# Value products of the last block in two 64-row halves, with a second PSUM bank of sums

## The chip, the cores and the metric

The kernel runs on one core of a Trainium2 chip. The metric is the device time of one execution in microseconds. The engines are named as in the profile: PE (TensorE, matrix products; PEld are its weight loads), DVE (VectorE), ACT (ScalarE), POOL (GpSimd) and SP (which issues DMAs). PSUM, into which PE writes, has eight banks; one bank holds 128 partitions of 512 float32 values, one tile of this kernel.

## The reference

Two attentions over 2048 positions with 32 heads of 18 columns, each with its own input and weights; their outputs stand side by side. A looks at eight positions, two apart, behind each position; B looks at all positions. The change touches B:

```python
qkv = (x @ wqkv).reshape(B, S, 3, H, Dh).transpose(2, 0, 3, 1, 4)
q, k, v = qkv[0], qkv[1], qkv[2]
scores = jnp.einsum("bhqd,bhkd->bhqk", q, k) * scale
p = _softmax(scores, axis=-1)
o = jnp.einsum("bhqk,bhkd->bhqd", p, v)
return o.transpose(0, 2, 1, 3).reshape(B, S, D) @ wo
```

All in float32. Many products of the kernel split their operands into a high and a low part of the faster type float32r and add three products; the value products (p times v) are plain float32, which makes two weight loads and two matmuls of one product.

## The kernel before

**Blocks and steps.** B's attention goes by groups of four heads (`g`, eight of them), blocks of 512 queries (`b`, four) and tiles of 128 keys (`kt`, 16). A step is one (g, b, kt): for each of the four heads, `score` (L219) makes a 128x512 tile of scores, keys on partitions (L226), and ACT makes its exponentials `e` (L232). While they last, maxima of later blocks are taken beside the scores (L156 on PE, L163 on DVE); for the last block there are none left to take.

**Value products.** `weigh` (L694) multiplies the exponentials with the values: for each head `i`, a product (L697) of the 128 keys' 19 columns (18 of the value and a column of ones, which sums the weights) with `e`, into partitions 32i to 32i+18 of the tile `po`. So four products stand in four column tiles of the array, and po collects 16 steps (`start` at kt 0, `stop` at kt 15). Partitions 32i+19 to 32i+31 are never written by PE; po is cleared once, far ahead (L658). In the last group and its last blocks, `weigh` is called for two steps at a time, at odd kt. At kt 15 it calls `finish`.

**What follows a block.** `finish` (L702) copies po to `o` on ACT (L706); for the last block it calls `closing` (L770) in place of that. In the last group the division by the sums is made on DVE: transpose in squares of 32, reciprocal, multiply, transpose back (`shortly` L739 for blocks 1 and 2, `inverse` L756 in `closing`). `closing` first makes the product that still lacks (`first(3, b, 1)`, L976), then two times `inverse` from po into o over 256 columns, and for each 128 columns a high part (ACT L779) and a low part (POOL L780); `end` multiplies with wo (L976), adds what had been summed before (L1036) and stores.

**Output products.** In the last block, PE also makes outputs of earlier blocks and parts of this block's. They are *quarters*: `sum_of` (L1009) lets `beside` (L987) make 288 columns for 128 positions in two halves of 64 rows, taken in turns and each with a PSUM bank of its own, 15 products a half (12 where the newest heads still lack), all at L1001. DVE then copies the first half's bank (L1020) and adds the second's (L1021). The list `waiting` holds them: one is made before `weigh` is called in a step, and another in even steps after the scores.

**Banks.** `bank()` gives the next bank of a ring: banks 0 to 3 for scores, 4, 5 and 6 for everything else, po is the eighth. A bank that is given again waits for the last reader of its tile. A quarter takes two banks of "else"; `first` takes one and keeps it until `end`.

**Order.** From L270 on the order of each engine's instructions is the order in which the program writes them. Nothing is moved; only waits on tiles hold an instruction back, and then everything behind it on its engine.

Of the kernel before, what the change touches and what calls it, by code (L numbers as in the profile page):

```python
# [7 lines left out]
F32 = mybir.dt.float32  # L8
F32R = mybir.dt.float32r
BF16 = mybir.dt.bfloat16  # L10
AF = mybir.ActivationFunctionType
# [11 lines left out]
NG = H // 4  # L23
NT = S // 128
NB = S // 512
# [34 lines left out]
def two_attentions(ctx: ExitStack, tc, xa, wa, woa, xb, wb, wob, out):  # L60
# [5 lines left out]
    nc = tc.nc  # L66
# [6 lines left out]
    p_bank = ctx.enter_context(tc.tile_pool(name="p_bank", bufs=1, space=PSUM))  # L73
# [3 lines left out]
    rings = {"all": list(range(7)), "scores": [0, 1, 2, 3], "else": [4, 5, 6]}  # L77
    ring = "all"

    def bank(kind=None):  # L80
        r = rings[kind or ring]
        r.append(r.pop(0))
        return p_bank.tile([128, 512], F32, name=f"bank{r[-1]}")
# [11 lines left out]
    po = p_po.tile([128, 512], F32, name="po")  # L95
# [141 lines left out]
    vs = {}  # L237
# [98 lines left out]
    with (tc.tile_pool(name="x", bufs=1, side="right") as xp,  # L336
# [103 lines left out]
        if True:  # L440
# [236 lines left out]
            es = []  # L677
# [13 lines left out]

    work = ctx.enter_context(tc.tile_pool(name="work", bufs=1, reuse_waits="tile"))
    ring = "else"
    def weigh(*steps):  # L694
        for g, b, kt, es in steps:
            for i in range(4):
                nc.tensor.matmul(po[32 * i : 32 * i + 19], vs[g][:, kt, 19 * i : 19 * i + 19], es[i],  # L697
                                 start=kt == 0, stop=kt == NT - 1)
        if kt == NT - 1:
            finish(g, b)  # L700

    def finish(g, b):  # L702
        o = work.tile([128, 512], F32, name="o", bufs=2)
        if g == NG - 1 and b == NB - 1:
            return closing(b, o, work.tile([128, 512], F32, name="rec", bufs=1))
        nc.scalar.activation(o, po, AF.Copy)  # L706
        den = work.tile([128, 16], F32, name="den", bufs=2)
        rec = work.tile([128, 512], F32, name="rec", bufs=1)
        parts = []

        def room():
            if g == NG - 1 and b == 0:

                parts[:] = [ap(work.tile([128, 4, 128], F32R, name=f"at{i}", bufs=1), (1, 512)) for i in range(2)]
            else:
                n = work.tile([128, 2, 512], F32R, name="n", bufs=1)
                parts[:] = n[:, 0], n[:, 1], n
            return parts

        if g == NG - 1 and b > 0:  # L720
            return shortly(b, o, rec, *room()[:2])

        def store():
            if g < NG - 1:
                load(do[:, g, :, 512 * b : 512 * b + 512].rearrange("i p n -> p i n"), parts[2].bitcast(F32))
            else:
                plan(step, full(b, parts))

        for at, f in ((1, lambda: load(den, o[DH:128:32])),
                      (8, lambda: nc.vector.reciprocal(den, den)),  # L730
                      (9, lambda: load(drec[g, b].rearrange("i (p n) -> (i p) n", n=16), den)),
                      (13, lambda: load(rec, rows(drec[g, b], (512, 4), (0, 32), (1, 512)))),
                      (18, lambda: nc.gpsimd.tensor_mul(o, o, rec)),  # L733
                      (19, lambda: nc.gpsimd.tensor_copy(room()[0], o)),
                      (20, lambda: nc.gpsimd.tensor_sub(parts[1], o, parts[0])),
                      (26, store)):
            later(at, f)
# [18 lines left out]
    def inverse(src, turned, cols, o):  # L756

        nc.vector.transpose(turned[:, cols], src[:, cols])
        divided(turned[:, cols])
        nc.vector.transpose(o[:, cols], turned[:, cols])  # L760

    def divided(square):

        n = square.shape[1] // 32
        inv = work.tile([128, 16], F32, name="den", bufs=2)[:, :n]
        each = ap(square, (32, n), (1, DH + 1))
        nc.vector.reciprocal(inv, ap(square[:, DH:], (32, n)))
        nc.vector.tensor_mul(each, each, ap(inv, (1, n), (0, DH + 1)))

    def closing(b, o, rec):  # L770

        n = work.tile([128, 2, 512], F32R, name="n", bufs=1)
        first(3, b, 1)
        for t in range(4):
            if t % 2 == 0:
                inverse(po, rec, slice(128 * t, 128 * t + 256), o)
            cols = slice(128 * t, 128 * t + 128)
            hi, lo = n[:, 0, cols], n[:, 1, cols]
            nc.scalar.activation(hi, o[:, cols], AF.Copy)  # L779
            nc.gpsimd.tensor_sub(lo, o[:, cols], hi)  # L780
        for t in range(4):
            end(t, b, (n[:, 0], n[:, 1]))
# [188 lines left out]
    def some(ps, t, h, c, hi, lo, start, stop):  # L971
        pos, cols = slice(128 * t, 128 * t + 128), slice(288 * h, 288 * h + 288)
        n = hi.shape[0]
        whi, wlo = wo["b"][c]
        for k, (a, w) in enumerate(((hi, whi), (hi, wlo), (lo, whi))):
            nc.tensor.matmul(ps, a[:, pos], w[:n, cols], start=start and k == 0, stop=stop and k == 2)  # L976
# [46 lines left out]
    def first(t, b, h):  # L1023
        sums[t, b, h] = bank()[:, :288]
        for c in range(4):
            some(sums[t, b, h], t, h, c, *olds[b][c], c == 0, False)
# [17 lines left out]
    def end(t, b, new):  # L1044
        for h in range(2):
            half_end(t, b, h, new)
        load(out[512 * b + 128 * t : 512 * b + 128 * t + 128, D:], ys[t, b])
# [75 lines left out]
    while step < ALL:  # L1123
        n, kt = divmod(step, NT)
        g, b = divmod(n, NB)
        places = positions(min(4 if behind() > 0 else 3, total - sum(given)))
        es = []
        for h in range(4):

            if inside and h == (3 if 3 in places else 2):  # L1130
                inside.pop(0)()
            es.append(score(g, b, kt, h, h in places))
        for fs in (behind_scores, outside):
            while fs:
                fs.pop(0)()

        paired = paired or kt % 2 == 0 and sum(given) == total
        for _ in range(1 if paired and step < ALL - 2 else len(waiting)):
            if waiting:
                waiting.pop(0)()  # L1140
        if ready and (kt % 2 == 0 or not paired):
            weigh(ready.pop(0))
        ready.append((g, b, kt, es))
        if paired and kt % 2:
            weigh(*ready)
            ready.clear()
        due()

        if len(waiting) > (0 if not paired else 2 if kt % 2 else len(waiting)):
            waiting.pop(0)()  # L1150
        step += 1
# [24 lines left out]
```

## Time and profile before

| | us |
|---|---|
| median of 3 runs | 1642.11 |
| lowest and highest run | 1640.54, 1644.94 |
| span of the profiled execution, first to last instruction | 1639.3 |
| busy in that span: PE, DVE, ACT, POOL | 1629.1, 1395.2, 1221.8, 959.4 |

The page gives the profiled execution's span and no whole time for it. A row of a view names line, engine, operation and tiles (written <- read); then, in a timeline, start and duration, and in brackets how long the engine had been idle and what released it. An `x4` merges four neighbours of one kind, with the duration of their union. Groups give busy time, mean nanoseconds of one, and idle time before them. "issue" stands for a wait that no semaphore explains. A matmul of 512 columns is shown with its whole way through the array, so neighbours overlap, and the distance between starts is what one costs.

### The profile page before, as it was taken

The page shows a single profiled execution, that of the slowest core. Times are in us where ns is not written, and L with a number is a line of the kernel's source. Part 1 is how long each engine was busy: PE and PEld are TensorE (multiplying, and loading weights), DVE is VectorE, ACT ScalarE, POOL GpSimd, SP SyncE. Part 2 cuts the span into 40 slices and gives each one's busy share as a digit, 9 for nine tenths or more (in the row PEclk, how much of TensorE's full clock was granted, in tenths as well). Part 3 has the DMA queues.
Part 4 walks back from the last instruction along what each step waited for, and adds up shares of the span by engine and source line. Part 5 has one row for each costly group of instructions (what it writes and reads, how often), then busy time and mean ns, then how long its engine had stood idle before and what let it go on. Part 6 is the DMA issues. An engine that isn't in the chain of part 4 may idle for free.

```text
span 1639.3 us, 33789 instructions
## 1 busy us (share of the span) xinstructions
PE 1629.1 (99%) x12906; PEld 952.7 (58%) x12906; DVE 1395.2 (85%) x2366; ACT 1221.8 (75%) x2419; POOL 959.4 (59%) x792
## 2 busy tenths in 40 slices
PE   9999999999999999999999999999999999999998
PEld 7999889999433444344344444344344344344676
DVE  5199999999899989989889989889889989888533
ACT  6424432111899998998998998998998998998554
POOL 2306642210365995994994994994995996930000
PEclk9999999999999999999999999999999999999999
DMA  8937954522222352164146135332632242033201
GB/s 250 238 116 204 266 158 140 136 86 90 46 64 58 75 139 82 41 139 109 39 101 150 35 95 121 90 83 69 121 97 65 51 125 62 21 115 130 95 38 59
DMA packets 186050, 172.01 MB, mean 105 GB/s; under 512 B 119152, under 2 KB 132976, under 8 KB 184160
## 3 DMA queue, kind: packets, MB, share of 16 engines
q1 hardware_dynamic: 181024, 158.31, 35.4%
q0 software_dynamic: 4032, 10.63, 3.1%
q8 instruction: 101, 1.65, 0.5%
q10 hardware_dynamic: 832, 0.92, 0.2%
q14 instruction: 61, 0.50, 0.1%
HBM read 96.94 MB, written 71.90 MB: 103 GB/s over the span
## 4 chain that ended last, share of the span: by engine, by line
PE 95%; DMA 2%; DVE 1%; POOL 1%; issue 0%; ACT 0%; SPq 0%; POOLq 0%; ACTq 0%; DVEq 0%
PE po L697 30%; PE bank L226 25%; PE bank L319 14%; PE bank L156 13%; PE bank L1001 7%; PE bank L256 5%; DMA raw<-xa 1%; POOL xlo L367 1%; DVE mx L163 1%; DMA dqk<-olo 0%; DMA dqk<-ohi 0%; PE bank L471 0%; DMA more<-xa 0%; DVE am L852 0%; DMA out<-y 0%
## 5 line engine op out<-in xcount | busy, mean ns | idle before, releaser
L163 DVE TENSOR_REDUCE mx<-bank 128x1 f32<-128x512 f32 x2048 | 1287.7, 684 | 142.9 <-PE bank L156 114.9
L232 ACT ACTIVATE e<-bank 128x512 f32<-128x512 f32 x2048 | 1059.9, 613 | 90.0 <-PE bank L226 50.3
L156 PE MATMUL bank<-ks,qs 54*128 54x512 f32 x2048 | 750.0, 422 | 1.1 <-DVE mx L163 0.9
L226 PEld LDWEIGHTS bank<-qs,ks 56*128 56x128 f32 x2048 | 331.1, 185 | 453.2 <-ACT e L232 423.0
L226 PE MATMUL bank<-qs,ks 56*128 56x512 f32 x2048 | 580.2, 425 | 0.0
L697 PE MATMUL po<-e,v 128*19 128x512 f32 x4096 | 537.4, 599 | 0.0
L156 PEld LDWEIGHTS bank<-ks,qs 54*128 54x128 f32 x2048 | 340.2, 184 | 9.7 <-DVE mx L163 4.7
L697 PEld LDWEIGHTS po<-e,v 128*19 128x19 f32 x4096 | 70.6, 97 | 182.0 <-issue 171.2
L834 POOL TENSOR_TENSOR pr<-aq,akv 128x1024 f32<-128x1024 f32 x72 | 158.4, 2201 | 15.5 <-PE bank L226 13.0
L877 POOL TENSOR_TENSOR pr<-lg,akv 128x1024 f32<-128x1024 f32 x72 | 158.3, 2198 | 0.6
L838 POOL TENSOR_TENSOR pr<-pr 128x1024 f32<-128x1024 f32 x64 | 152.4, 2382 | 5.0
L647 ACT ACTIVATE ohi<-bank 128x512 f32<-128x512 f32 (+1 forms) x56 | 30.4, 596 | 150.1 <-issue 115.2
L319 PE MATMUL bank<-xhi,ahi 64*128 64x512 f32 (+1 forms) x448 | 114.5, 387 | 0.0
L319 PE MATMUL bank<-xhi,alo 64*128 64x512 f32 (+1 forms) x448 | 113.5, 387 | 0.0
L319 PE MATMUL bank<-xlo,ahi 64*128 64x512 f32 (+1 forms) x448 | 113.1, 388 | 0.1
L878 POOL TENSOR_TENSOR pr<-pr 128x512 f32<-128x512 f32 x72 | 92.3, 1282 | 5.6
L367 POOL TENSOR_TENSOR alo<-raw,ahi 128x512 fp32r<-128x512 f32 (+1 forms) x14 | 17.6, 1257 | 121.5 <-ACT ahi L366 87.8
L459 POOL TENSOR_TENSOR olo<-olo,ohi 128x512 fp32r<-128x512 f32 x36 | 46.1, 1293 | 67.3 <-ACT ohi L458 61.5
L733 POOL TENSOR_TENSOR o<-o,rec 128x512 f32<-128x512 f32 x29 | 37.3, 1286 | 53.9 <-DMA rec<-drec 47.5
L319 PEld LDWEIGHTS bank<-xhi,ahi 64*128 64x128 f32 (+1 forms) x448 | 65.8, 181 | 1.4
L319 PEld LDWEIGHTS bank<-xhi,alo 64*128 64x128 f32 (+1 forms) x448 | 64.9, 182 | 1.3
L319 PEld LDWEIGHTS bank<-xlo,ahi 64*128 64x128 f32 (+1 forms) x448 | 64.4, 182 | 1.9 <-POOL xlo L367 0.5
(197 smaller groups left out, 1795.5 us busy)
## 6 DMA issues: line engine op xcount, KB each, us to landing
do<-n SPq DMA_DIRECT2D x28, 512.0 KB
da<-ohi SPq DMA_DIRECT2D x52, 256.0 KB
akv<-da SPq DMA_DIRECT2D x64, 175.5 KB
out<-y SPq DMA_DIRECT2D x32, 288.0 KB
qs<-dqk SPq DMA_DIRECT2D x30, 288.0 KB
ks<-dqk SPq DMA_DIRECT2D x30, 288.0 KB
at<-dao SPq DMA_DIRECT2D x64, 128.0 KB
rec<-drec SPq DMA_DIRECT2D x29, 256.0 KB
```

Of the source, the lines that this page charges most:

```text
L156: nc.tensor.matmul(ps, qs[at, b, p, 128 * t : 128 * t + 128], ks[at, p, 512 * k : 512 * k + 512], start=True, stop=True)
L163: nc.vector.tensor_reduce(mx[:, r, p, t, k : k + 1], ps, axis=AX.X, op=ALU.max)
L226: nc.tensor.matmul(ps, ks[at, p, 128 * kt : 128 * kt + 128], qs[at, b, p], start=True, stop=True)
L232: nc.scalar.activation(e, ps, AF.Exp, scale=SCALE)
L256: nc.tensor.matmul(ps, a, b, start=c == i == 0, stop=c == 4 and i == 1)
L319: nc.tensor.matmul(ps, a, b, start=start, stop=stop)
L697: nc.tensor.matmul(po[32 * i : 32 * i + 19], vs[g][:, kt, 19 * i : 19 * i + 19], es[i], start=kt == 0, stop=kt == NT - 1)
L834: nc.gpsimd.tensor_mul(pr, ap(st["q"][:, 2 * c], (SUB, 2), (0, W), (1, SUB)), window(st["k"], c))
L838: nc.gpsimd.tensor_add(st["pr"], st["pr"], pr)
L877: nc.gpsimd.tensor_mul(at, ap(st["lg"], (0, 2), (SUB, W), (1, SUB)), window(st["v"], c))
L878: nc.gpsimd.tensor_add(at[:, :, :4], at[:, :, :4], at[:, :, 4:])
L1001: nc.tensor.matmul(ps, a, b, start=start, stop=stop)
```

## The change

In the last block of the last group (`last`), each value product is made as two, one of rows (keys) 0 to 63 and one of rows 64 to 127. The first goes to po, the second to a second tile of sums at the same partitions. That tile is bank 6: at the first call for this block it is taken out of the ring "else", which keeps two banks, and is cleared by DVE. In `closing`, ACT copies po to o, DVE adds the second tile to o, and `inverse` reads o where it read po. In all other blocks the loop over `(po, *other_po)` has one turn with all 128 rows, as before.

```diff
+    other_po = []
     def weigh(*steps):
         for g, b, kt, es in steps:
+            last = g == NG - 1 and b == NB - 1
+            if last and not other_po:
+                rings["else"].remove(6)
+                other_po.append(p_bank.tile([128, 512], F32, name="bank6"))
+                nc.vector.memset(other_po[0], 0.0)
             for i in range(4):
-                nc.tensor.matmul(po[32 * i : 32 * i + 19], vs[g][:, kt, 19 * i : 19 * i + 19], es[i],
-                                 start=kt == 0, stop=kt == NT - 1)
+                for r, to in enumerate((po, *other_po)):
+                    at = slice(64 * r, 64 * r + 64) if last else slice(0, 128)
+                    nc.tensor.matmul(to[32 * i : 32 * i + 19], vs[g][at, kt, 19 * i : 19 * i + 19], es[i][at],
+                                     start=kt == 0, stop=kt == NT - 1)
...
         first(3, b, 1)
+        nc.scalar.activation(o, po, AF.Copy)
+        nc.vector.tensor_add(o, other_po[0], o)
         for t in range(4):
             if t % 2 == 0:
-                inverse(po, rec, slice(128 * t, 128 * t + 256), o)
+                inverse(o, rec, slice(128 * t, 128 * t + 256), o)
```

## The prediction

> **What bounds the kernel now.** I read the page first: span, engines, share of the chain.
>
> ```profile
> span 1639.3 us, 33789 instructions
> PE 1629.1 (99%) x12906; PEld 952.7 (58%) x12906; DVE 1395.2 (85%) x2366; ACT 1221.8 (75%) x2419; POOL 959.4 (59%) x792
> PE 95%; DMA 2%; DVE 1%; POOL 1%; issue 0%; ACT 0%; SPq 0%; POOLq 0%; ACTq 0%; DVEq 0%
> ```
>
> PE is both the busiest engine and 95% of the chain, so a microsecond that PE waits or works more is a microsecond of time. The change touches the last block only, so next I asked for the value products (L697) from its first one on, and for the chain in one pair of its steps and at its end.
>
> ```profile
> L697 PE MATMUL po<-e,v x128: 592/592/607, 1571.8 to 1627.7; 128*19 128x512 f32 x128
> ```
>
> ```profile
> 1612.43 1.84 PE po L697 x16
> 1614.27 0.66 PE bank L226 x2
> 1614.93 1.99 PE bank L1001 x29
> 1616.92 0.49 PE bank L226 x4
> 1617.41 2.32 PE bank L1001 x29
> ...
> 1624.71 1.78 PE bank L976 x12
> 1626.49 1.96 PE po L697 x16
> ```
>
> The 64 products of the block are 128 PE instructions (two passes each), in 8 calls of `weigh` that take two steps each: 16 instructions, 1.84 us. A pair of steps is a chain of PE alone: `weigh`, four scores (L226), one output quarter (L1001), four scores, a second quarter. The second quarter takes 2.32 us where the first takes 1.99; the cause of that matters below.
>
> **The value products themselves.** PE's weight loads around two of the calls, behind the last product of the quarter before the first of them:
>
> ```profile
> 1619.44 0.29 PE L1001 MATMUL bank<-qs,n 64*128 64x288 f32 x1
> ...
> 1619.66 0.14 PEld L697 LDWEIGHTS po<-e,v 128*19 128x19 f32 x8 [0.16 <-issue]
> 1620.10 0.12 PEld L697 LDWEIGHTS po<-e,v 128*19 128x19 f32 x4 [0.31 <-issue]
> 1620.53 0.12 PEld L697 LDWEIGHTS po<-e,v 128*19 128x19 f32 x4 [0.31 <-issue]
> 1621.50 0.30 PEld L226 LDWEIGHTS bank<-qs,ks 56*128 56x128 f32 x4 [0.85 <-issue]
> ...
> 1626.42 0.13 PEld L697 LDWEIGHTS po<-e,v 128*19 128x19 f32 x8 [0.16 <-issue]
> ...
> 1628.26 0.19 PEld L976 LDWEIGHTS bank<-qs,pr 126*128 126x128 f32 x1 [0.85 <-issue]
> ```
>
> Four tiles of 32 columns run beside each other, one pass every 0.43 us (1620.10 to 1620.53), four passes a call. The change makes eight instructions per pass: four column tiles in two halves of 64 rows. Each half moves as many columns as the full depth did, so what counts is whether the halves run beside each other. No row shows that for these tiles. The nearest: L1001 is made of 64-row halves, 30 instructions of 288 columns in 1.99 us, 0.133 us a pair, while 12 full-depth ones of the same width (L976) take 1.78, 0.148 each. Two halves cost what one full product costs. So I take the passes as unchanged, plus the start of four more tiles: four loads of 0.10 us end within 0.12, so some 7 ns a tile, 0.03 us a call, **+0.2** for eight calls. Bounds: below, a half passes in half the time (rival 3, -6.9); above, the halves run one after the other, 16 steps x 2 passes x 0.43 = +13.8. Between them lies issue: L1001's 60 instructions in 1.99 us are 33 ns each, and a call will have 64, 2.12 us for 1.84 now, +2.3 in all.
>
> The Trainium skill ("TensorE: Matmul & The Clock Gate", measured speedup vs the span model) has a figure against the change: four row tiles of 512 columns gave 3.07 times one tile's rate, not 4. Worked out from it as an estimate, the 14.7 us of eight calls would take 4/3.07 of that, +4.5 us, and the sum would be +12.9; the L1001 and L976 rows show no such loss for two halves.
>
> **Drains.** Around a call PE's loads stop: 0.16 us before, 0.85 after. Scores after `weigh` take 0.66 us, after a quarter 0.49, so leaving costs about 0.17; entering costs 0.09 (1619.44 to 1619.66 is 0.22, against 0.133 between L1001's pairs). If halves of 64 rows beside halves of 64 rows needed no drain, 7 of 8 calls would save 0.26: -1.8. But at 1626.42 and 1628.26 `weigh` stands between L976 products, which use the array's depth as it does (126 rows) and differ from it in columns alone, and the idle times are the same 0.16 and 0.85. A change of columns alone drains too, and 64x128 to 64x32 is that. I take **0**, and keep -1.8 as the lower end.
>
> **The memset, once.** The new sums' bank 6 is cleared on DVE when the first call (1571.78) is written, and PE's second product needs it. What DVE has in its queue then:
>
> ```profile
> 1571.67 0.77 DVE L752 STREAM_TRANSPOSE o<-rec 128x256 f32<-128x256 f32 x2
> 1571.78 0.14 PEld L697 LDWEIGHTS po<-e,v 128*19 128x19 f32 x8 [0.16 <-issue]
> ...
> 1572.37 0.42 DVE L1020 COPY y<-bank 128x288 f32<-128x288 f32 x1
> ...
> 1572.89 0.46 DVE L1021 TENSOR_TENSOR y<-bank,y 128x288 f32<-128x288 f32 x1
> ```
>
> ```profile
> 1575.53 0.46 DVE L1020 COPY aohi<-bank 128x288 f32<-128x288 f32 x1 [2.18 <-PE bank L1001]
> ```
>
> ```profile
> L658 DVE MEMSET po<- x1: 485/485/485, 55.5 to 55.5; 128x512 f32 x1
> ```
>
> The order is written by hand: transposes of the block before, both evictions of the quarter just made, then the memset. L1021 ends at 1573.35; the memset of the same shape took 0.485, so bank 6 is clear at about 1573.87 and PE goes on at 1573.93 (a DVE end reaches PE after 0.05, next part). The call would have started at 1571.78: **+2.15**. The first half-product of po runs meanwhile, but the seven other tiles need their passes all the same. Behind the wait stand the rest of the call, a quarter and the scores, so ACT's exponentials come later too; DVE has 2.18 us of idle time behind it, so nothing is late on that side. Bounds: 1.6 if the memset gets ahead of L1021, 2.4 with slower hand-offs.
>
> **The ring of banks, eight times.** `rings["else"].remove(6)` leaves two banks for the quarters, and a quarter takes two. Between two quarters with only scores between them:
>
> ```profile
> 1609.65 0.46 DVE L1020 COPY y<-bank 128x288 f32<-128x288 f32 x1 [3.58 <-PE bank L1001]
> ...
> 1609.91 0.65 PE L1001 MATMUL bank<-qs,wohi 64*128 64x288 f32 x2
> 1610.16 0.18 PEld L1001 LDWEIGHTS bank<-qs,wohi 62*128 62x128 f32 x1 [0.29 <-DVE y L1020]
> ...
> 1610.21 0.46 DVE L1021 TENSOR_TENSOR y<-bank,y 128x288 f32<-128x288 f32 x1
> ```
>
> ```profile
>   PEld bank L1001: 2.3, 8
> ```
>
> With three banks the second quarter's first half has a free bank (start 1609.91); its second half needs the bank that L1020 empties: 1610.11, and PE goes on at 1610.16, 0.05 later. That is the missing third of a microsecond in the 2.32. The last row is the same wait summed, asked of L1020 from 1573.6 to 1624.9: 8 times, 0.29 each. With two banks the first half needs the bank of L1020 and the second half that of L1021, which ends at 1610.67 instead of 1610.11. Each of the eight waits grows by 0.56: **+4.5**. Where a `weigh` stands between quarters, its 1.84 us cover both evictions (1.0 us); without that cover those would wait as well. The `first` that follows a quarter directly takes one bank:
>
> ```profile
> 1624.25 0.46 DVE L1020 COPY y<-bank 128x288 f32<-128x288 f32 x1 [3.59 <-PE bank L1001]
> ...
> 1624.64 0.19 PEld L976 LDWEIGHTS bank<-qs,pr 126*128 126x128 f32 x1 [0.24 <-issue]
> ```
>
> Its bank comes free at 1624.71, PE at 1624.76 for 1624.64: **+0.1**. Bounds of the ring: 0 if the banks don't come round as I read it, 5.5 with a refill after each stall.
>
> **The end.** Now DVE transposes po itself. Afterwards ACT copies po to o, then DVE adds bank 6, and the transposes read o.
>
> ```profile
> 1564.77 0.60 ACT L706 ACTIVATE o<-po 128x512 f32<-128x512 f32 x1 [2.52 <-issue]
> ```
>
> ```profile
> 1628.48 0.45 DVE L758 STREAM_TRANSPOSE rec<-po 128x256 f32<-128x256 f32 x1 [3.21 <-PE po L697]
> ```
>
> ```profile
> L163 DVE TENSOR_REDUCE mx<-bank 128x1 f32<-128x512 f32 x2048 | 1287.7, 684 | 142.9 <-PE bank L156 114.9
> ```
>
> The copy starts about where the transpose does (1628.48) and takes 0.60. The add is 128x512 out of PSUM: 0.68 by L163, 0.81 by L1021's 0.46 for 288 columns scaled; I take 0.69, nearer the same shape. With two hand-offs of 0.05 the transposes start 1.4 us later. ACT has nothing queued ahead; behind the add stand the transposes, and everything that follows waits for them: **+1.4** (1.2 to 1.7).
>
> **The sum.** 0.2 + 0 + 2.15 + 4.5 + 0.1 + 1.4 = +8.35 us on a span of 1639.3. The median of the runs, 1642.11, lies 2.8 above that span (the page gives no whole time for the profiled execution); I let what lies around the span stand: 1642.1 + 8.4 = 1650.5.
>
> **Rivals.**
> 1. The halves do not fully run beside each other. For it: no row shows eight tiles of two halves in two-pass products. Against: the L1001 halves. It gives more than the issue bound, up to one half after the other: 1642.1 + 8.4 + 2.3 to 13.8, so 1653 to 1664. The chance is 0.12.
> 2. One of the two waits is not there (the memset is done in time, or the ring gives no wait more): +6.2 or +3.8, so 1648.3 or 1645.9. For it: the profile shows neither wait as it will be. Against: DVE works in order, and the eight waits are in the trace. Chances 0.04 and 0.06.
> 3. Not slower: a pass of a 64-row half takes 0.21 us in place of 0.43. For it: L226's 64-row pairs move 512 columns in 0.245 (four in 0.49). It would save 32 passes x 0.215 = 6.9 of the 8.4: 1643.6. It decides from 0.32 a pass (8.4 - 3.5 = 4.9). Against: L976 at full depth moves its columns as fast as half pairs do, so depth isn't what makes a value pass slow; the two passes per product are. Chance 0.05.
>
> **How the numbers follow.** My forecast holds 0.73: with its bounds (drains gone -1.8, issue +2.3) 1648.5 to 1653. Leaving out most of rival 1 (0.1) and rival 3 (0.05), the range for 8 in 10 is 1645.5 to 1656. What can be told from no change is 0.3%, 4.9 us, so slower begins at 1647.0. Slower: the forecast, rival 1 and the first case of rival 2, less 0.03 for the scatter of the medians, 0.86; the same: the second case of rival 2, most of rival 3 and that scatter, 0.11; faster: 0.03, for rival 3 with drains and a wait gone as well.
>
> **What would show it.** Right: 256 instructions of L697's line in the last block in two banks with eight starts within some 50 ns and passes still 0.43 apart; a wait of PE of about 2 us for a MEMSET at the block's first call; eight waits of L1001 of about 0.85 put down to L1021; the first transpose of the end 1.4 us further behind the last value product. Wrong: calls much over 1.9 us (rival 1) or under 1.5 (rival 3), scores after a call in 0.49 (no drain), waits that still name L1020.

## The result and the profile after

The changed kernel takes 1648.58 us (median of 5 runs, 1647.62 to 1649.96) against 1642.11 before (1639.87 to 1644.94): a ratio of 1.0044, 95% interval 1.0031 to 1.0058, so 5 to 9.5 us slower. The spans of the two profiled executions differ by 8.5 us. The page of the changed kernel, span and engines:

```profile
span 1647.8 us, 34049 instructions
PE 1633.5 (99%) x13034; PEld 949.7 (58%) x13034; DVE 1396.6 (85%) x2368; ACT 1222.3 (74%) x2420; POOL 959.1 (58%) x792
```

PE has 128 matmuls more, and its busy time grew by 4.4 us of the 8.5. That is no measure of the work added: the page of experiment 1, which adds no matmul, has 1632.6 us busy, 3.5 more than before, so a part of what PE waits is shown as busy. The value products of the last block (`weigh`'s matmul is L706 here), asked of their line over that stretch:

```profile
L706 PE MATMUL po<-e,v x128: 589/589/604, 1571.7 to 1635.0; 64*19 64x512 f32 x128
...
L706 PE MATMUL bank<-e,v x128: 589/589/603, 1573.9 to 1635.0; 64*19 64x512 f32 x128
```

The split is made: 256 instructions of 64 rows, half of them into the second bank. Two things can be read off the starts alone. The first and the last product of po start 63.3 us apart where it was 55.9, and the second bank's first product comes 2.2 us after po's.

**The first call.** The timeline of DVE and PE around it, in order of start:

```profile
1571.65 0.11 PEld L706 LDWEIGHTS po<-e,v 64*19 64x19 f32 x2 [0.16 <-issue]
1571.65 1.03 PE L706 MATMUL po<-e,v 64*19 64x512 f32 x2
...
1572.77 0.46 DVE L1032 TENSOR_TENSOR y<-bank,y 128x288 f32<-128x288 f32 x1
...
1573.33 0.48 DVE L702 MEMSET bank<- 128x512 f32 x1
...
1573.87 0.09 PEld L706 LDWEIGHTS bank<-e,v 64*19 64x19 f32 x1 [2.11 <-DVE bank L702]
```

PE makes one product of po (the x2 are its two passes), then stands until the memset is done, and the memset stands behind the add of the quarter before.

**Between quarters.** One place, the counterpart of the one shown before (the L1020 and L1021 of before are L1031 and L1032):

```profile
1607.69 0.46 DVE L1031 COPY y<-bank 128x288 f32<-128x288 f32 x1 [3.58 <-PE bank L1012]
...
1608.21 0.18 PEld L1012 LDWEIGHTS bank<-qs,wohi 64*128 64x128 f32 x1 [0.36 <-DVE y L1031]
...
1608.26 0.46 DVE L1032 TENSOR_TENSOR y<-bank,y 128x288 f32<-128x288 f32 x1
...
1608.77 0.18 PEld L1012 LDWEIGHTS bank<-qs,wohi 62*128 62x128 f32 x1 [0.38 <-DVE y L1032]
```

The second quarter's first half now waits for the copy, its second half for the add: PE goes on 0.05 us behind the end of L1032, not of L1031. The chain of waits of the changed kernel shows the same as steps of DVE in what was a chain of PE alone (start, duration, what):

```profile
1613.56 2.03 PE bank L1012 x30
1615.59 0.46 DVE y L1031
...
1616.14 0.47 DVE y L1032
...
1616.65 2.26 PE bank L1012 x27
```

**The calls themselves.** PE's weight loads around one call, and the starts of PE's matmuls in its first two passes:

```profile
1618.84 0.09 PEld L706 LDWEIGHTS po<-e,v 64*19 64x19 f32 x1 [0.16 <-issue]
...
1619.29 0.10 PEld L706 LDWEIGHTS po<-e,v 64*19 64x19 f32 x1 [0.29 <-issue]
...
1619.72 0.10 PEld L706 LDWEIGHTS po<-e,v 64*19 64x19 f32 x1 [0.29 <-issue]
...
1620.71 0.30 PEld L226 LDWEIGHTS bank<-qs,ks 56*128 56x128 f32 x4 [0.85 <-issue]
```

```profile
1618.85 0.60 PE L706 MATMUL po<-e,v 64*19 64x512 f32 x1
...
1618.89 0.60 PE L706 MATMUL bank<-e,v 64*19 64x512 f32 x1
1619.29 0.59 PE L706 MATMUL po<-e,v 64*19 64x512 f32 x1
...
1619.34 0.59 PE L706 MATMUL bank<-e,v 64*19 64x512 f32 x1
```

Passes are 0.43 us apart, as with full depth, with eight tiles in each that start within 50 ns. The idle times on both sides are 0.16 and 0.85, as before: 64-row halves beside 64-row halves did not save the drain.

**The end.** DVE's timeline behind the last call:

```profile
1636.37 0.69 DVE L784 TENSOR_TENSOR o<-bank,o 128x512 f32<-128x512 f32 x1 [4.00 <-ACT o L783]
1637.09 0.45 DVE L767 STREAM_TRANSPOSE rec<-o 128x256 f32<-128x256 f32 x1
```

The last call ends (next PE start) at 1635.50, so the transposes start 1.59 us behind it; before it was 1628.48 behind 1628.26, 0.22.

**An account of the last block.** The part of the kernel ahead of the block is the same code in all of them, save for the step or two in which experiments 2, 4, 5 and 6 begin, but it ends at different times in different executions: the first call starts anywhere from 1569.7 to 1574.9 us in the ten profiles of this study. So I read the experiments from that start to the end of the span, cut at the starts of the calls and of the instruction behind each (PE's timeline, us):

| kernel | first call | 7 other calls | between calls | behind the last | sum |
|---|---|---|---|---|---|
| before | 1.84 | 12.90 | 41.74 | 11.01 | 67.49 |
| changed | 4.08 | 13.07 | 46.70 | 12.31 | 76.16 |
| e1_ring_only | 1.84 | 12.90 | 46.35 | 11.00 | 72.09 |
| e2_clear_early | 1.87 | 13.06 | 46.97 | 12.30 | 74.21 |
| e3_no_add | 4.08 | 13.06 | 46.70 | 10.98 | 74.83 |
| e4_two_engines_evict | 3.03 | 13.07 | 42.41 | 12.23 | 70.73 |
| e5_costs_undone | 1.87 | 13.07 | 42.41 | 12.16 | 69.50 |
| e6_before_two_engines | 1.84 | 12.90 | 41.67 | 10.89 | 67.30 |
| e7_halves_in_turn | 4.05 | 13.06 | 46.71 | 12.30 | 76.13 |
| e8_one_more_on_dve | 4.21 | 13.06 | 46.38 | 12.30 | 75.95 |

Changed less before: 2.24 + 0.17 + 4.96 + 1.30 = 8.67 us. Each row is one execution, but stretches that a kernel leaves as they are repeat closely: 46.70, 46.70 and 46.71 between the calls of the changed kernel and of experiments 3 and 7.

### The profile page after: what moved, and what is told of

Read it like the earlier page. It is cut to its first block, busy times and chain, and to the rows that moved or that the text cites. A ratio compares the mean times of both kernels' runs of the same rounds, so it can differ in the third digit from the quotient of the medians.

```text
span 1647.8 us, 34049 instructions
## 1 busy us (share of the span) xinstructions
PE 1633.5 (99%) x13034; PEld 949.7 (58%) x13034; DVE 1396.6 (85%) x2368; ACT 1222.3 (74%) x2420; POOL 959.1 (58%) x792
## 4 chain that ended last, share of the span: by engine, by line
PE 92%; DMA 2%; DVE 2%; POOL 2%; issue 1%; ACT 0%; SPq 0%; POOLq 0%; DVEq 0%; ACTq 0%
PE po L706 30%; PE bank L226 25%; PE bank L156 13%; PE bank L319 12%; PE bank L1012 7%; PE bank L256 5%; DMA raw<-xa 2%; POOL xlo L367 1%; DMA dqk<-olo 1%; DVE mx L163 1%; POOL olo L459 0%; PE bank L471 0%; DVE y L1032 0%; DVE y L1031 0%; PE bank L706 0%
## 5 line engine op out<-in xcount | busy, mean ns | idle before, releaser
L226 PEld LDWEIGHTS bank<-qs,ks 56*128 56x128 f32 x2048 | 331.2, 185 | 453.3 <-ACT e L232 423.0
L226 PE MATMUL bank<-qs,ks 56*128 56x512 f32 x2048 | 580.1, 425 | 0.0
L706 PE MATMUL po<-e,v 128*19 128x512 f32 (+1 forms) x4096 | 538.6, 599 | 0.0
L706 PEld LDWEIGHTS po<-e,v 128*19 128x19 f32 (+1 forms) x4096 | 71.1, 96 | 180.9 <-issue 170.4
L319 PEld LDWEIGHTS bank<-xlo,ahi 64*128 64x128 f32 (+1 forms) x448 | 63.3, 182 | 2.4 <-POOL xlo L367 0.5
```

The source lines that it names most:

```text
L226: nc.tensor.matmul(ps, ks[at, p, 128 * kt : 128 * kt + 128], qs[at, b, p], start=True, stop=True)
L319: nc.tensor.matmul(ps, a, b, start=start, stop=stop)
L706: nc.tensor.matmul(to[32 * i : 32 * i + 19], vs[g][at, kt, 19 * i : 19 * i + 19], es[i][at], start=kt == 0, stop=kt == NT - 1)
```

## The experiments

The ratio of each experiment is to runs of the kernel before that were taken beside it, not to the 1642.11 of above: their medians are 1640.61 us (18 runs) for experiments 1 to 4 and 1640.67 us (21 runs) for 5 to 8.

**1. The ring alone.** The kernel before, which loses bank 6 and does nothing with it:

```diff
         for g, b, kt, es in steps:
+            if g == NG - 1 and b == NB - 1 and 6 in rings["else"]:
+                rings["else"].remove(6)
```

> The kernel before, with bank 6 taken out of the ring at the last block's first value products and nothing else. Theory (waits): each of the eight waits between neighbouring quarters grows from 0.29 to 0.85 us and names the add L1021 in place of the copy L1020, and the one ahead of the single product sums grows by 0.12, so the span is 4.6 us over the 1639.3 of before, about 1643.9. If the third of a microsecond by which one quarter of the changed kernel came later still is part of the ring, it shows here too (4.9). Rival (the halves are what costs): no change, within 0.5 us.

Measured: 1645.47 us, ratio 1.0029 (1.0017 to 1.0040); the last block 72.09, 4.60 more than before, all of it between the calls. One place between two quarters, from the timeline of DVE and PE, and then who waited for the add, asked of its line (L1023 in this kernel) and of L1021 in the kernel before:

```profile
1604.50 0.46 DVE L1022 COPY y<-bank 128x288 f32<-128x288 f32 x1 [3.56 <-PE bank L1003]
1605.02 0.18 PEld L1003 LDWEIGHTS bank<-qs,wohi 64*128 64x128 f32 x1 [0.37 <-DVE y L1022]
...
1605.07 0.46 DVE L1023 TENSOR_TENSOR y<-bank,y 128x288 f32<-128x288 f32 x1
...
1605.58 0.18 PEld L1003 LDWEIGHTS bank<-qs,wohi 62*128 62x128 f32 x1 [0.38 <-DVE y L1023]
```

```profile
  PEld bank L1003: 3.9, 9
  PE bank L1003: 1.3, 8
```

```profile
  PEld bank L1001: 0.8, 1
```

PE's matmuls wait eight times for the add, which none did before. The wait comes in two parts, 0.37 us for the copy and 0.38 for the add, with the first half's first product between them, and not as the single 0.85 of the expectation. The ring costs what was forecast, without any split. The changed kernel's 4.96 between the calls has 0.35 more than this kernel's 4.61; that is not the ring.

**2. The memset out of the way.** The bank is taken and cleared a step earlier, ahead of the transposes in DVE's queue. It is the bank given last, so the next quarter takes the two that it would have taken.

```diff
-                rings["else"].remove(6)
...
-                nc.vector.memset(other_po[0], 0.0)
...
-                for r, to in enumerate((po, *other_po)):
+                for r, to in enumerate((po, *other_po) if last else (po,)):
...
+        if step == ALL - NT:
+            taken = rings["else"].pop()
+            other_po.append(p_bank.tile([128, 512], F32, name=f"bank{taken}"))
+            nc.vector.memset(other_po[0], 0.0)
         due()
```

> The changed kernel, with the memset written one step earlier, ahead of the transposes of the block before, in the bank that the next quarter does not need. Theory: PE no longer waits for the memset, which takes 2.2 us off; the evictions behind it on DVE end 0.49 later and hold the next quarter by some 0.26. So about 1.95 us under the changed kernel's 1647.8, near 1645.9, and the first call of value products takes 1.87 like the others. Rival (the first call is long for its own sake, as the first in a new tiling): it stays near 4 us and the time stays.

Measured: 1646.46 us, ratio 1.0034 (1.0021 to 1.0047); the last block 74.21, 1.95 less than the changed kernel. Timeline of DVE and PE:

```profile
1571.09 0.48 DVE L1157 MEMSET bank<- 128x512 f32 x1 [0.18 <-DVE y L1028]
...
1572.60 0.09 PEld L702 LDWEIGHTS po<-e,v 64*19 64x19 f32 x1 [0.16 <-issue]
...
1572.60 0.09 PEld L702 LDWEIGHTS bank<-e,v 64*19 64x19 f32 x1
```

Both halves start at once, and the first call takes 1.87 as the others do. The 2.2 us were the place of the memset in DVE's queue; between the calls 0.27 us came back: the evictions on DVE end later, and in the trace the next quarter now waits 0.21 for the add.

**3. Without the copy and the add.** `inverse` reads po again, so the sums over keys 64 to 127 of the block are left out of the output.

```diff
-        nc.scalar.activation(o, po, AF.Copy)
-        nc.vector.tensor_add(o, other_po[0], o)
...
-                inverse(o, rec, slice(128 * t, 128 * t + 256), o)
+                inverse(po, rec, slice(128 * t, 128 * t + 256), o)
```

> The changed kernel without the copy and the add ahead of the last division: the sums over keys 64 to 127 of the last block are left out of the output. Theory: the end is a chain of DVE, so 1.3 to 1.4 us go, near 1646.4. Rival (the copy and the add hide behind the twelve products that PE makes meanwhile): no change.

Measured: 1647.88 us, ratio 1.0040 (1.0025 to 1.0055). By runs that says little, being within their scatter; the stretch behind the last call says it: 10.98 us for 12.31, and before it was 11.01. The copy and the add cost 1.3 us of the end, hidden by nothing.

**4. Both banks emptied at once.** In the last block only:

```diff
+        if step >= ALL - NT:
+            y2 = work.tile([128, 288], F32, name="y2", bufs=1)
+            nc.vector.tensor_copy(y, one)
+            nc.scalar.activation(y2, two, AF.Copy)
+            nc.gpsimd.tensor_add(y, y, y2)
+            return
         nc.vector.tensor_copy(y, one)
         nc.vector.tensor_add(y, two, y)
```

> The changed kernel, with a quarter's two banks emptied at the same time in the last block: DVE copies the first, ACT the second into another tile, POOL adds the two. Theory: both banks are free 0.5 us after the quarter, as only the first was, so the eight waits fall from 0.85 to about 0.3 each and 4.4 us go, near 1643.4. Rival (PE waits there for another reason than the second bank): the waits stay at 0.85 and the time at 1647.8.

Measured: 1644.34 us, ratio 1.0023 (1.0013 to 1.0032); the last block 70.73, 5.4 less than the changed kernel. The three instructions of one quarter, from the timeline:

```profile
1608.72 0.46 DVE L1033 COPY y<-bank 128x288 f32<-128x288 f32 x1 [2.41 <-PE bank L1012]
1608.78 0.41 ACT L1034 ACTIVATE y<-bank 128x288 f32<-128x288 f32 x1 [0.46 <-PE bank L1012]
1609.31 0.80 POOL L1035 TENSOR_TENSOR y<-y,y 128x288 f32<-128x288 f32 x1 [2.04 <-ACT y L1034]
```

After the first call PE's weight loads waited 3.3 us for the copies and 4.2 us for the adds in the changed kernel; here they wait 3.7 us for the copies and not at all for the second bank. Between the calls 4.3 us went, of the 4.4 expected from the waits, and 0.35 of that is the late add of experiment 8; another 1.05 went at the first call, which I had not put in the expectation: the add that stood ahead of the memset on DVE is gone from there. With two banks and this way of emptying them, the stretches between the calls are 0.7 us over those of before.

**5. All costs taken down.** Experiments 2 and 4 together, and the end in two parts:

```diff
-        nc.scalar.activation(o, po, AF.Copy)
-        nc.vector.tensor_add(o, other_po[0], o)
         for t in range(4):
             if t % 2 == 0:
+                two = slice(128 * t, 128 * t + 256)
+                if t == 0:
+                    for c in (two, slice(256, 512)):
+                        nc.scalar.activation(o[:, c], po[:, c], AF.Copy)
+                nc.vector.tensor_add(o[:, two], other_po[0][:, two], o[:, two])
                 inverse(o, rec, slice(128 * t, 128 * t + 256), o)
```

> The changed kernel with all three costs taken down together: memset a step earlier, a quarter's banks emptied by two engines, and the copy and add of the end made in two parts of 256 columns, so that the first transposes start after half of them. Theory (the halves themselves cost 0.02 us a call and nothing else): from the first call of the block to the end 69.2 to 69.7 us, against 67.49 before and 76.16 in the changed kernel; the calls take 1.87. Rival (something of the halves themselves is still in the 8.7): 71 or more. Faster than before would need drains that go; not expected.

Measured: 1643.10 us, ratio 1.0013 (1.0004 to 1.0021); the last block 69.50. Of the 2.0 us that are left over before, the end holds 1.15, the stretches between the calls 0.67, the calls 0.19. Nothing larger hides in the halves, and they gain nothing either. The two parts of the end saved 0.15 only: the first transposes come earlier, but the second add stands in DVE's queue between two `inverse`.

**6. The kernel before with the emptying of experiment 4.** The same edit of `sum_of` in the kernel before.

> The kernel before with the two-engine emptying of banks in the last block alone. Theory: the eight waits of 0.29 stay, since the copy that they wait for starts and ends as before (the bank waited for is the first half's): from the first call to the end 67.2 to 67.9, no change. Rival (the ACT copies get in the way of the exponentials, or free the banks earlier): over 68.5, or under 66.5.

Measured: 1640.89 us, ratio 1.0004 (0.9995 to 1.0013); the last block 67.30, between the calls 41.67 for 41.74. With three banks the add is off the path, so taking it from DVE is worth nothing; with two it is worth 4 us (4.3 in experiment 4, less the late add). None of these kernels beats the one before.

**7. The halves in turn.**

```diff
-            for i in range(4):
-                for r, to in enumerate((po, *other_po)):
+            for r, to in enumerate((po, *other_po)):
+                for i in range(4):
```

> The changed kernel with the order of the halves turned round: all four heads of rows 0 to 63, then all four of rows 64 to 127. If the tiles of the array take their work independently of the order, a call stays at 1.87 and the time as in the changed kernel. If PE starts products strictly in the order written, the second half's tiles start behind the first's second pass: at least 0.4 us more a call, 3 us or more in all.

Measured: 1649.24 us, ratio 1.0048 (1.0033 to 1.0063); the calls 1.87, the block 76.13. PE's weight loads in one call:

```profile
1622.02 0.12 PEld L706 LDWEIGHTS po<-e,v 64*19 64x19 f32 x6 [0.16 <-issue]
...
1622.06 0.12 PEld L706 LDWEIGHTS bank<-e,v 64*19 64x19 f32 x6
1622.46 0.12 PEld L706 LDWEIGHTS po<-e,v 64*19 64x19 f32 x4 [0.29 <-issue]
1622.49 0.12 PEld L706 LDWEIGHTS bank<-e,v 64*19 64x19 f32 x4
```

The second bank's tiles do not wait for the first one's second pass, though they are written behind it. The order of the tiles within a call does not matter.

**8. One more instruction on DVE.** The 0.35 us that experiment 1 left over sit in one add of the changed kernel, from DVE's timeline:

```profile
1580.90 0.46 DVE L1031 COPY y<-bank 128x288 f32<-128x288 f32 x1 [2.24 <-PE bank L1012]
1581.81 0.46 DVE L1032 TENSOR_TENSOR y<-bank,y 128x288 f32<-128x288 f32 x1 [0.46 <-PE bank L226]
```

Every other such add starts 0.10 behind its copy, this one 0.46 (the scores named as releaser do not write its bank), and the next quarter waits for it. It is the same add, with the same 0.46, in experiments 2, 3 and 7; in experiment 1 it has its 0.10.

```diff
-                nc.vector.memset(other_po[0], 0.0)
+                nc.vector.memset(other_po[0][:, :256], 0.0)
+                nc.vector.memset(other_po[0][:, 256:], 0.0)
```

> The changed kernel with the memset written as two of 256 columns, so that every later instruction of DVE stands one place further back. It asks of the 0.35 us by which one add (the second quarter after the first call) starts late. If that belongs to a place in DVE's instruction stream, the add starts 0.10 after its copy, as all others do, and the next instruction in the stream may be late in its place where DVE is idle anyway. If it belongs to that quarter's data or banks, the add stays 0.46 behind. The first call grows by some 0.1.

Measured: 1650.84 us, ratio 1.0059 (1.0045 to 1.0072), with the first call of its profile at 1573.9 and not 1571.7; the last block 75.95, 0.2 less than the changed kernel: the first call 0.13 longer, the stretches 0.32 shorter. The same two instructions in this kernel:

```profile
1583.28 0.46 DVE L1032 COPY y<-bank 128x288 f32<-128x288 f32 x1 [2.24 <-PE bank L1013]
1583.84 0.46 DVE L1033 TENSOR_TENSOR y<-bank,y 128x288 f32<-128x288 f32 x1
```

Counted from the start of the trace, as the page counts DVE's instructions, the late add is number 2326 in all four; the same add is 2325 in experiment 1 and 2327 here. So the delay goes with a place in DVE's instruction stream and not with the quarter, as far as this one run can show it. What DVE does at that place no run shows; that stays open.

## Why the prediction was right

Its terms stand one to one in the account of the last block.

- **Halves**, forecast +0.2: 0.024 us a call, 0.19 in eight. They run beside each other wholly. The estimate of +4.5 us from the Trainium skill ("TensorE: Matmul & The Clock Gate", measured speedup vs the span model) does not hold for two halves here: a call went from 1.843 to 1.867.
- **Drains**, forecast 0: idle 0.16 and 0.85 us as before, shown by the trace. The argument was the right one: `weigh` between products of full depth had had the same idle times. The Trainium skill ("TensorEngine Tiling (Array Packing)", key properties) has the same rule: a change of the tiling mode drains the array. The Trainium skill (same page, available configurations) lists 64x128 and 64x32 as two modes.
- **Memset**, forecast +2.15: 2.22 (2.24 less the call's 0.02), shown by experiment 2. The forecast left out most of the 0.10 us between the end of the add and the start of the memset.
- **Ring**, forecast +4.5 and +0.1: 4.61 in experiment 1, shown; experiment 4 takes it away by another way. The sign that was named for it, eight waits of about 0.85 put down to the add, came in another form: 0.36 for the copy and 0.38 for the add at each place.
- **End**, forecast +1.4: the transposes start 1.37 later, the end comes 1.30 later, and experiment 3 takes back 1.3.

What was not forecast is the 0.35 of one late add. With it the terms come to 8.67, and the span to 8.5, since the first call stood 0.13 earlier in the profiled execution.

The time itself came out 1.9 us under the forecast of 1650.5, inside the range. That is scatter of executions, and one loose step. I took the 2.8 us between the profiled span and the median of before for what lies around a span. The profiled execution of the changed kernel, span 1647.8, took 1649.58 in all, 1.8 more, and so it is, within 0.1, in the later runs of the kernel before; so the span of before was that of an execution about 1 us faster than its median. The profiled execution of the changed kernel was 1.0 slower than its own. Together they make the 2.0 by which the spans differ more (8.5) than the medians (6.5). The runs of one kernel spread over 2 to 6 us, the part ahead of the last block over 5; that the medians fell this near to the forecast is luck in part, and the account of the block is the better check.

Two small slips in the working change nothing: 1650.5 less 1.8 is 1648.7 and not 1648.5, and the score halves (L226) have 56 rows, not 64.

Rival 1 (halves one after the other) falls by the calls of 1.87, rival 3 (a half pass in half the time) by the 0.43 between passes, rival 2 by experiments 1 and 2, each of which shows one of the waits alone.

## What to carry to other kernels

Work that is split to fill an array needs a place for its second sums, and that place was someone's buffer: before a bank is taken from a ring, see in the trace which wait the ring still had, and to which later release it will move. An initialisation on an in-order queue costs what is queued ahead of it besides its own half microsecond (2.2 us here); write it where nobody waits for that engine. And an array that was full already gained nothing from more tiles: passes stayed 0.43 us apart with four tiles or eight.

## What the runs showed of the hardware

- Eight tiles of 64 rows by 32 columns run beside each other in two-pass float32 products, with starts some 7 ns apart (eight from 1618.85 to 1618.89) and the pass time of four full-depth tiles, 0.43 us.
- The matmuls of different tiles do not start in the order written. Both passes of one product stand ahead of the next product: at the first call, where the memset held the second product, PE made two matmuls of the first (the x2 of 1.03 us) and nothing else. Yet in the other calls the first passes of all eight tiles start within 50 ns, and second passes 0.43 us later; experiment 7 shows the same in the other order. The Trainium skill ("TensorE: Matmul & The Clock Gate", the mechanism) says that matmuls start strictly in order; the traces here do not agree.
- One DVE instruction started 0.35 us late at the same place of the stream in four profiles (0.46 us behind the instruction before it, where 0.10 is usual), and the same add at its normal time once one more instruction stood ahead of it.
